# A new order for the opening of a sparse-attention and feed-forward kernel

## The chip, the cores and the metric

The kernel runs on one core of one Trainium2 chip. The metric is the device time of one execution in microseconds (us). A core has five engines that run side by side, each taking its own instructions in order: TensorE (PE, matrix products; loading its weights is shown apart as PEld), VectorE (DVE), ScalarE (ACT), GpSimd (POOL) and SyncE (SP, which here only issues transfers). Transfers are issued from SP's, ACT's and POOL's queues and carried by the same 16 DMA engines. PE writes its products into PSUM, eight banks per partition; everything else lies in SBUF.

## The reference

Eight batches, eight heads, 576 tokens, 64 channels a head. A token attends to those within 32 positions of it; eight global tokens are seen by all and see all. The result, 4608 tokens by 512 channels, goes through a two-layer network.

```python
scores = scale * np.matmul(q, k.transpose(0, 1, 3, 2))
mask = np.abs(pos[:, None] - pos[None, :]) <= window
mask = mask | is_global[:, None] | is_global[None, :]
attn = softmax of scores where mask, else -1e9
x = np.matmul(attn, v), heads side by side   # 4608 x 512
h = x @ w_in                                 # 512 -> 2048
out = (h * np.cos(h)) @ w_out                # 2048 -> 512
```

## The kernel before

**Pairs and units.** The attention is done by pairs of heads, 32 in all; pairs 2s and 2s+1 make half batch s, four pairs a batch. The network is done by tiles of 512 tokens, nine of them. A first-layer unit (`mlp_in`, L754, then `mlp_act`, L765) is four matmuls for 128 of the 2048 inner channels, a cosine on ACT and a product g on DVE; a second-layer unit (`mlp_out`, L790) is four of the sixteen matmuls for 128 tokens. A tile has 16 units of either layer; the fourth of each second-layer group copies its bank out and stores it. That makes 288 units.

**A pair** passes these steps. `k` and `q` (L598, L609): transposes on PE into a bank, and for pairs 0 to 3 small products that pick the global tokens (`pick_globals`, L307), copied out by ACT. `s` (L621 for pairs 0 to 9, L689 for the rest): scores on PE, exponentials on ACT, mask product pm on DVE. `p` (L641, L710): values on PE into pv, of which there is one, then sums, reciprocals and normalised rows xn on DVE. `x` (L670, L734): xn is transposed on PE, DVE copies it into xT, and after a batch's fourth pair POOL writes the eight global columns (L687). `y` (L404): the value rows of the global tokens, from one-hot products, copied by ACT.

**Written order.** The order of all instructions is written out by hand as strings of steps. FRONT covers pairs 0 to 9; MID, FIFTH, SIXTH and ORDER each cover a half batch from number 4 on, issuing the steps of its pairs (letters a, z) and the copies of the next one (c, d); in MID, which stands right behind FRONT, only copies, masks and units. `1` asks for a first-layer unit, `2` for a second-layer unit, `m` and `t` for the two halves of a first-layer unit. A request yields nothing where no unit may run: `one` (L869) needs a ready tile (`ready`: two tiles after FRONT, a third after half batch 5), `two` (L879) needs its inputs and a count below `outs_by`. Other steps: `L` loads a half batch's k and q through POOL, `M` its v through SP, `C` casts v on POOL, `W` loads a quarter of w_in, `O` w_out, `E`, `Y`, `A` gather the global rows, `H` and `g` place them, `f` and `w` are matmuls that only fill time, `n` sums squares on ACT, `Z` builds the steady masks on DVE, `K` casts a half batch from memory to memory, `V` and `U` hold POOL ahead of such a cast until a pair's data is there, `B` (`bring`) transposes k and q and loads v for a half batch through SP.

**Banks.** PSUM banks are taken by tags, each used round by round: s has three, h two, o one, pv two. `k`, `q`, `y` and first-layer units use h; between a `+` and a `-` of the strings every third and fourth first-layer unit uses s. Scores use three of s and the one of o in the opening (`front`), later one of h.

**Half batches 0 to 4** are loaded by POOL with a cast to fp16 (`load_qk`, L275, into three buffers, the third lying in the place of w_out), v as float32 into the two buffers that later hold the products g of tiles 0 and 1. From half batch 5 on everything comes through `K` and `B`. In the loop behind MID, second-layer units are allowed up to 8 (s - 3), and behind the last pair (tail) the remaining units of both layers alternate.

Of the kernel before, what the change touches and what calls it, by code (L numbers as in the profile page):

```python
# [19 lines left out]
P = 128  # L20
NP = H // 2
QB = 56
NB = 11
# [181 lines left out]
def kernel(  # L205
# [31 lines left out]
    nc.sync.dma_start(gidx_all, dview(gi, 0, (0, P), (1, 2 * G)))  # L237
    nc.sync.dma_start(gidx_col, dview(gi, 0, (0, 16), (2, G), (1, 1)))
    nc.sync.dma_start(gidx_row, dview(gi, 0, (2 * G, 1), (1, 2 * G)))
# [67 lines left out]
    def pick_globals(pr, t, src, ones, n, to):  # L307
# [5 lines left out]
        nc.scalar.copy(to, view(t, (0, to.shape[1]), (1, G)))  # L313
# [61 lines left out]

    def next_values(s):

        nc.vector.memset(vn_of(s)[0:64, 0], 0.0)
        load_vn(s)
# [18 lines left out]
    def cast_vn(s):  # L398
        if s > 1:
# [4 lines left out]
    def value_rows(s, part):  # L404

        hs = slice(2 * part, 2 * part + 2)
        rows = ps.tile([P, 512], FP32, tag="h", bufs=2, name="rows")
        for t in range(NK5):
            nc.tensor.matmul(rows[0:G, 0 : 2 * D], one_v[:, t], vn16(s)[:, t, hs, 0:D], start=t == 0, stop=t == NK5 - 1)
        nc.scalar.copy(vn16(s)[0:G, :, hs, 0:D], view(rows[0:G], (0, NK5), (D, 2), (1, D)))  # L410
# [187 lines left out]
    def local_k(pr):  # L598
        to = kw[pr % NK][:, :, G:]
        if pr < 2 * HY:  # L600
            t, g = turned(kn[pr // 2 % NN], pr, KP)
            if pr < PK:
                pick_globals(pr, g, kn[pr // 2 % NN], one_k, KP, k5(pr)[:, :, 0:G])
            nc.scalar.copy(k5(pr)[:, :, G:].rearrange("p n (j r) -> p n j r", r=RW),
                           view(t, (KS // RW, NK5), (1, KS // RW), (QP, RW)))
# [3 lines left out]
    def local_q(pr):  # L609
        to = qb[pr % NK][:, :, G:]  # L610
        if pr < 2 * HY:
            t, g = turned(qn[pr // 2 % NN], pr, QP)
            if pr < PK:
                pick_globals(pr, g, qn[pr // 2 % NN], one_q, QP, q5(pr)[:, 1:, 0:G])
            nc.scalar.copy(qb[pr % NK][:, 0, 0:G], t[:, :, 0])
            nc.scalar.copy(q5(pr)[:, :, G:].rearrange("p n (j r) -> p n j r", r=RW),
                           view(t[:, :, 1:], (KS // RW, NK5), (1, KS // RW), (QP, RW)))
        else:
            nc.vector.tensor_copy(to, view(qT[pr // 2 % 2][:, pr % 2], (QB, NB), (1, QB)))  # L619

    def scores5(pr):  # L621
        kp, qp = k5(pr), qb[pr % NK].rearrange("p j c -> p (j c)")
        pm = pm_of[pr] = work.tile([P, 2 * CN], FP16, tag="pm", name="pm")
        tags = (("s", 3), ("s", 3), ("s", 3), ("o", 1))
# [7 lines left out]
        for h in range(2):  # L632
            e = work.tile([P, 2 * CB], FP16, tag="e", bufs=3)
            nc.scalar.activation(e[:, 0:CA], st[h][:, 0:CA], AF.Exp, scale=scale)  # L634
            nc.vector.tensor_tensor(pm[:, h * CN : h * CN + CA], e[:, 0:CA], mask5[:, 0:CA], ALU.mult)
        e = work.tile([P, 2 * CB], FP16, tag="e", bufs=3)
        for h in range(2):
            nc.scalar.activation(e[:, h * CB : (h + 1) * CB], st[2 + h][:, 0:CB], AF.Exp, scale=scale)  # L638
        nc.vector.tensor_tensor(view(pm[:, CA:], (CN, 2), (1, CB)), view(e, (CB, 2), (1, CB)), view(mask5[:, CA:], (0, 2), (1, CB)), ALU.mult)  # L639
# [49 lines left out]
    def scores(pr):  # L689
# [10 lines left out]
        for h in range(2):  # L700
            e = work.tile([P, 2 * CB], FP16, tag="e", bufs=3)
# [387 lines left out]
```

## Time and profile before

| what | value |
|---|---|
| runs | 353.09, 354.77, 355.42 us; median 354.77 |
| span of the profiled execution, its only time on the page | 353.2 us |
| PE, DVE, ACT, POOL busy | 332.5, 250.1, 245.9, 108.5 us |
| granted PE clock over the span | 0.983 |
| opening, to the end of pair 9's transposes | 58.76 us |
| DMA | 44.58 MB, 126 GB/s on average |

The page gives each engine's busy time; groups of instructions by line, with count, busy time, mean length of one and the idle time ahead of them; who waited for whom; a chain of waits that leads to the last instruction; and a timeline. Stretches of the span can be asked for by themselves. A line of the timeline begins with the start in us and the length, then engine, line of the code, operation, output and input, and in brackets how long the engine stood idle and who released it. Instructions of the same kind that follow on one another are drawn together, with their count.

### The profile page before, as it was taken

To read this page: it belongs to the slowest core of one execution; us is meant where nothing else is said; L and a number is where in the kernel's file an instruction comes from. 1 tells how busy PE (TensorE), PEld (TensorE's weight loads), DVE (VectorE), ACT (ScalarE), POOL (GpSimd) and SP (SyncE) were. 2 spreads that over 40 slices of the span, in tenths; PEclk is the share of its full clock that TensorE was granted. 3 is DMA by queue.
4 is the path that set the end of the run, shared out by engine and by line. 5 is a ranking of instruction groups with operands and counts; after the bars stand their busy time and mean duration, and the time that the engine had idled before them with its cause. 6 is when DMAs were issued, how large, how long until landed. Compare 5 with 4: busy or idle time off the path is not lost.

```text
span 353.2 us, 8389 instructions
## 1 busy us (share of the span) xinstructions
PE 332.5 (94%) x3169; PEld 170.9 (48%) x3169; DVE 250.1 (71%) x611; ACT 245.9 (70%) x423; POOL 108.5 (31%) x221
## 2 busy tenths in 40 slices
PE   7887789999986999999999999999999999999993
PEld 3566675444443444544444545454544444444442
DVE  6565888887586778778787979697878466556410
ACT  8778987884754877777878787777878856644300
POOL 8854847434070507050705071416000100000000
PEclk9898989999999999999999999999999999999998
DMA  5999993999999999999999999999980000100112
GB/s 82 186 149 165 167 192 41 207 164 132 165 147 160 146 199 135 178 118 194 143 187 139 183 139 176 135 161 153 179 93 32 31 32 30 60 32 30 58 63 68
DMA packets 165891, 44.58 MB, mean 126 GB/s; under 512 B 153764, under 2 KB 160996, under 8 KB 165668
## 3 DMA queue, kind: packets, MB, share of 16 engines
q1 hardware_dynamic: 105860, 26.70, 51.2%
q0 software_dynamic: 59984, 17.28, 50.5%
q8 instruction: 27, 0.44, 0.5%
q14 instruction: 20, 0.16, 0.2%
HBM read 44.41 MB, written 19.17 MB: 180 GB/s over the span
## 4 chain that ended last, share of the span: by engine, by line
PE 73%; ACT 8%; DVE 5%; DMA 5%; issue 4%; SPq 3%; POOL 1%; ACTq 0%; POOLq 0%; DVEq 0%
PE po L800 32%; PE ph L762 30%; PE tx L744 2%; DMA kn<-in_k_dram 2%; PE st L699 2%; ACT e L702 2%; PE pv L719 2%; ACT e L634 1%; DMA vw<-vg 1%; ACT e L707 1%; SPq L414 1%; PE po L782 1%; ACT e L638 1%; DVE xn L666 1%; DVE pm L639 1%
## 5 line engine op out<-in xcount | busy, mean ns | idle before, releaser
L762 PE MATMUL ph<-xT,w_in 128*128 128x512 f16 x576 | 140.3, 379 | 1.1 <-DVE g L769 0.3
L768 ACT ACTIVATE cos<-ph,pio 128x512 f16<-128x512 f32 x144 | 97.1, 687 | 62.1 <-PE ph L762 59.9
L800 PE MATMUL po<-w_out,g 128*128 128x512 f16 x560 | 135.4, 379 | 0.0
L769 DVE TENSOR_TENSOR g<-cos,ph 128x512 f16<-128x512 f16 x144 | 95.9, 685 | 42.9 <-ACT cos L768 41.7
L762 PEld LDWEIGHTS <-w_in 128*128 128x128 f16 x576 | 54.2, 97 | 64.6 <-issue 4.6
L800 PEld LDWEIGHTS <-g 128*128 128x128 f16 x560 | 53.7, 98 | 63.6
L703 DVE TENSOR_TENSOR pm<-e,mask 128x512 f16<-128x512 f16 x44 | 18.8, 426 | 19.0 <-ACT e L702 17.7
L702 ACT ACTIVATE e<-st 128x512 f16<-128x512 f32 x44 | 23.9, 594 | 10.0 <-PE st L699 9.8
L980 POOL COPY gate<-xn 1x1 f16<-1x1 f16 x8 | 1.4, 180 | 87.9 <-DVE xn L730 87.9
L752 POOL COPY xT<-xg 128x4 f16 x48 | 15.6, 325 | 32.5 <-DVE xT L747 29.9
L272 POOL DMA_DIRECT2D q<-in_q_dram x11 | 24.0, 2182 | 0.0
L818 ACT ACTIVATE xn<-xn 128x1536 f16<-128x1536 f16 (+1 forms) x16 | 22.5, 1407 | 0.0
L730 DVE TENSOR_TENSOR xn<-pv,r_all 128x768 f16<-128x768 f32 x22 | 21.1, 958 | 1.0
L805 ACT COPY o<-po 128x512 f32<-128x512 f32 x17 | 10.0, 586 | 14.7 <-PE po L800 14.3
L807 DVE COPY o<-po 128x512 f32<-128x512 f32 x18 | 12.4, 690 | 9.0 <-PE po L800 8.5
L272 POOL DMA_DIRECT2D k<-in_k_dram x11 | 18.1, 1645 | 0.9 <-issue 0.9
L768 ACT ACT_TABLE_LOAD x12 | 15.4, 1283 | 0.2
L719 PE MATMUL pv<-vw,pm 128*64 128x65 f16 x484 | 12.7, 197 | 2.7 <-DMA vw<-vg 2.7
L607 DVE COPY kw<-kT 128x1320 f16<-128x1320 f16 x22 | 15.1, 685 | 0.0
L702 ACT ACT_TABLE_LOAD x11 | 14.1, 1283 | 0.2
L699 PEld LDWEIGHTS <-kw 64*128 64x128 f16 x484 | 8.4, 95 | 10.7 <-issue 8.1
L699 PE MATMUL st<-qb,kw 64*128 64x64 f16 x484 | 11.2, 191 | 1.5 <-DVE qb L619 1.1
(185 smaller groups left out, 385.9 us busy)
## 6 DMA issues: line engine op xcount, KB each, us to landing
out_dram<-o SPq DMA_DIRECT2D x35, 256.0 KB
vw<-v SPq DMA_DIRECT2D x32, 165.0 KB
v<-in_v_dram POOLq DMA_DIRECT2D x11, 288.0 KB
k<-in_k_dram POOLq DMA_DIRECT2D x11, 288.0 KB
q<-in_q_dram POOLq DMA_DIRECT2D x11, 288.0 KB
vn<-in_v_dram SPq DMA_DIRECT2D x20, 120.0 KB
w_in<-in_moe_w_in_dram POOLq DMA_DIRECT2D x4, 512.0 KB
w_out<-in_moe_w_out_dram POOLq DMA_DIRECT2D x1, 2048.0 KB
```

Source lines behind the costliest of these rows:

```text
L272: nc.gpsimd.dma_start(dst[s].rearrange("t (h d) -> t h d", h=4), dview(src, base, (D, S), (S * D, 4), (1, D)))
L699: nc.tensor.matmul(st[j // 8 * 2 + h][:, j % 8 * C : j % 8 * C + C], kp[hp, j], qp[hp, j], start=True, stop=True)
L702: nc.scalar.activation(e[:, 0:512], st[h], AF.Exp, scale=scale)
L703: nc.vector.tensor_tensor(view(pm[:, h], (1, 512)), e[:, 0:512], view(mask, (1, 512)), ALU.mult)
L719: nc.tensor.matmul(pv[r0 : r0 + C, j // 6, c0 : c0 + 65], pm[:, h, j], vp[:, j, h], start=True, stop=True)
L730: nc.vector.tensor_tensor(view(xn, (384, 2), (D, 6), (1, D)), view(pv, (512, 2), (65, 6), (1, D)), view(rp, (6, 2), (1, 6), (0, D)), ALU.mult)
L752: nc.gpsimd.tensor_copy(xT[:, :, bass.ds(pool_idx[g] + b * S, 1)], xg[:, :, g : g + 1])
L762: nc.tensor.matmul(ph, w_in16[:, j, f * P : (f + 1) * P], xT[:, j, t * TT : (t + 1) * TT], start=(j == 0), stop=(j == NC - 1))
L768: nc.scalar.activation(cos, ph, AF.Sin, bias=pio2)
L769: nc.vector.tensor_tensor(g, cos, ph, ALU.mult)
L800: nc.tensor.matmul(po, g16[:, f, s * P : (s + 1) * P], w_out16[:, f], start=(f == 0), stop=(f == NF - 1))
L818: nc.scalar.activation(view(xn, (BP * P, 2), (1, n)), view(xn, (BP * P, 2), (1, n)), AF.Square, accum_out=x_sq[:, s : s + 1])
```

## The change

The new opening works in another order and shares its work out differently.

- Half batch 0's k and q come as float32 through SP's and ACT's queues, ahead of the global indices, into `vn32[0]`, and are cast by DVE (k of pairs 0 and 1), ACT (q of pair 0) and POOL (q of pair 1). v of half batches 0 and 1 is loaded at the start; all v loads now share the two places of `vn32[1]`, so each next one follows a cast (`r`).
- FRONT: pairs 0 and 1 are transposed ahead of the first scores; the quarters of w_in (W0 to W3) are issued between pairs 1 and 4, ahead of L3; w_out (`O`) follows pair 5. Sixteen first-layer units (all of tile 0) stand behind pair 5's values, with k, q of pairs 6 and 7 among them; then pairs 6 and 7; then tile 0's sixteen second-layer units, with pairs 8 and 9 among them. Small buffers and the first mask are filled at steps `b`.
- Value rows once per half batch (`value_rows`): one copy of 256 columns by ACT, repeated by POOL. k copies of odd pairs go from ACT to DVE, the eight-column q copy too. The first two mask products of a pair become one.
- MID, FIFTH, SIXTH and ORDER stay; `outs_by` becomes 8 (s - 2), 16 at first.
- In the tail the squares of w_in use places of xn in turn.

```diff
-FRONT = ("M1 s0 E0 C0 E1 L2 k1 q1 w4 s1 y0.0 f4 k2 q2 C1 H0 p0 M2 L3 y0.1 s2 k3 q3 f2 x0 p1 M3 H1 g4 g5 g6 C2 y1.0 s3 g7 L4 I k4 q4 f2 x1 p2 M4 y1.1 s4 "
-         "C3 W0 k5 q5 f2 x2 p3 y2.0 s5 g8 g9 W1 W2 W3 k6 q6 f2 x3 p4 y2.1 s6 C4 Y0 k7 q7 f2 x4 p5 n0 y3.0 s7 k8 q8 f2 x5 p6 y3.1 s8 H2 k9 q9 f2 x6 p7 y4.0 s9 "
-         "x7 p8 y4.1 O m m x8 K5 p9 t t + m m t t x9 -")
+FRONT = ("k1 q1 b0 s0 w4 E0 b2 C0 r2 y0 b3 s1 L2 b4 k2 q2 w2 p0 b1 E1 k3 q3 s2 f2 x0 p1 C1 r3 y1 H0 H1 W0 g4 g5 C2 r4 g6 I "
+         "s3 k4 q4 f2 x1 p2 W1 g7 s4 k5 q5 f2 x2 p3 y2 W2 s5 f2 x3 W3 L3 p4 m m x4 p5 t t 1 1 C3 O g8 g9 1 1 x5 1 1 y3 1 1 1 L4 k6 q6 1 1 k7 q7 1 1 1 F0 s6 s7 "
+         "f2 n0 p6 C4 f2 p7 x6 Y0 H2 x7 2 2 2 2 K5 y4 2 2 k8 q8 2 2 k9 q9 s8 2 2 2 2 s9 p8 2 2 x8 2 2 p9 x9")
...
     def vn_of(s):
-        i = s if s < 4 else 2
-        return view(vn32[i // 2][:, 4 * (i % 2)], (4 * D, NK5), (1, 4 * D))
+        return view(vn32[1][:, 4 * (s % 2)], (4 * D, NK5), (1, 4 * D))
+
+    def load_first(eng, src, pr):
+        to = first_k(pr)[KPAD:KP] if src is k else first_q(pr)
+        eng.dma_start(to, dview(src, 2 * pr * S * D, (RW * D, S // RW), (S * D, 2), (1, RW * D)))
...
-    def value_rows(s, part):
-        hs = slice(2 * part, 2 * part + 2)
+    def value_rows(s):
+        rows, vp = ps.tile([P, 512], FP32, tag="h", bufs=2, name="rows"), vn16(s)
         for t in range(NK5):
+            nc.tensor.matmul(rows[0:G, 0 : 4 * D], one_v[:, t], vp[:, t, :, 0:D], start=t == 0, stop=t == NK5 - 1)
+        nc.scalar.copy(vp[0:G, 0, :, 0:D], view(rows[0:G], (D, 4), (1, D)))
+        nc.gpsimd.tensor_copy(vp[0:G, 1:, :, 0:D], ...)
...
+            copy = nc.vector.tensor_copy if pr % 2 else nc.scalar.copy
...
-        for h in range(2):
-            e = work.tile([P, 2 * CB], FP16, tag="e", bufs=3)
-            nc.scalar.activation(e[:, 0:CA], st[h][:, 0:CA], AF.Exp, scale=scale)
-            nc.vector.tensor_tensor(pm[:, h * CN : h * CN + CA], e[:, 0:CA], mask5[:, 0:CA], ALU.mult)
+        for i, (c, n) in enumerate(((0, CA), (CA, CB))):
+            e = work.tile([P, 2 * CA], FP16, tag="e", bufs=3)
+            for h in range(2):
+                nc.scalar.activation(e[:, h * n : (h + 1) * n], st[2 * i + h][:, 0:n], AF.Exp, scale=scale)
+            nc.vector.tensor_tensor(view(pm[:, c:], (CN, 2), (1, n)), view(e, (n, 2), (1, n)), view(mask5[:, c:], (0, 2), (1, n)), ALU.mult)
...
+        for t in ((k, nc.sync), (q, nc.scalar)):
+            load_first(t[1], t[0], 0)
+        nc.sync.dma_start(gidx_all, dview(gi, 0, (0, P), (1, 2 * G)))
+        nc.sync.dma_start(gidx_col, dview(gi, 0, (0, 16), (2, G), (1, 1)))
+        load_first(nc.scalar, q, 1)
+        load_first(nc.sync, k, 1)
...
+        cast_first(nc.vector.tensor_copy, k, 0)
+        cast_first(nc.scalar.copy, q, 0)
+        cast_first(nc.gpsimd.tensor_copy, q, 1)
         build_band()
+        cast_first(nc.vector.tensor_copy, k, 1)
+        build_ones()
         index_rows(1)
...
-            outs_by[0] = 8 * (s - 3)
+            outs_by[0] = 8 * (s - 2)
```

More of the change, by code (lines that the diff above doesn't have):

```diff
@@ L402, in cast_vn @@
         nc.gpsimd.tensor_copy(new[:, :, :, 0:D], old)
-    def value_rows(s, part):
-        hs = slice(2 * part, 2 * part + 2)
-        rows = ps.tile([P, 512], FP32, tag="h", bufs=2, name="rows")
+    def value_rows(s):
+        rows, vp = ps.tile([P, 512], FP32, tag="h", bufs=2, name="rows"), vn16(s)
         for t in range(NK5):
-            nc.tensor.matmul(rows[0:G, 0 : 2 * D], one_v[:, t], vn16(s)[:, t, hs, 0:D], start=t == 0, stop=t == NK5 - 1)
-        nc.scalar.copy(vn16(s)[0:G, :, hs, 0:D], view(rows[0:G], (0, NK5), (D, 2), (1, D)))
+            nc.tensor.matmul(rows[0:G, 0 : 4 * D], one_v[:, t], vp[:, t, :, 0:D], start=t == 0, stop=t == NK5 - 1)
+        nc.scalar.copy(vp[0:G, 0, :, 0:D], view(rows[0:G], (D, 4), (1, D)))
+        first = vp[0:G, 0, :, 0:D]
+        nc.gpsimd.tensor_copy(vp[0:G, 1:, :, 0:D], bass.AP(first.tensor, first.offset, [first.ap[0], [0, NK5 - 1], *first.ap[1:]]))
     def load_vg(pr):
@@ L700, in scores @@
         for h in range(2):
-            e = work.tile([P, 2 * CB], FP16, tag="e", bufs=3)
+            e = work.tile([P, 2 * CA], FP16, tag="e", bufs=3)
             nc.scalar.activation(e[:, 0:512], st[h], AF.Exp, scale=scale)
             nc.vector.tensor_tensor(view(pm[:, h], (1, 512)), e[:, 0:512], view(mask, (1, 512)), ALU.mult)
-        e = work.tile([P, 2 * CB], FP16, tag="e", bufs=3)
+        e = work.tile([P, 2 * CA], FP16, tag="e", bufs=3)
         n = (NB - 8) * C
@@ L824, in weight_squares @@
         if j == 0:
[L825 to L826 removed]
+            w_sq[c] = view(work.tile([P, 2, BP, P], FP16, tag="xn", bufs=4, name="wsq"), (512, 3), (1, 512))
+        at = w_sq[c][:, (0, 1, 2, 1)[j]]
+        nc.scalar.activation(at, w_in16[:, j, c * 512 : (c + 1) * 512], AF.Square)
         if j:
[L828 removed]
+            nc.vector.tensor_tensor(w_sq[c][:, 0], w_sq[c][:, 0], at, ALU.add)
     def weight_norms(c):
@@ L885, in two @@
                 mlp_out(*outs_q.pop(0))
-    outs_by = [0]
+    outs_by = [16]
     ready = [0, 0]
```

106 lines of the change are left out of this document (57 added, 49 removed).

## The prediction

> **What bounds the kernel now.** First the head of the page: TensorE (PE) is busy for 94% of the span. Then busy time by stage, cut where a pair's scores begin, and where the opening ends (58.76, the end of pair 9's transposes in the chain of waits).
>
> ```profile
> span 353.2 us, 8389 instructions
> PE 332.5 (94%) x3169; PEld 170.9 (48%) x3169; DVE 250.1 (71%) x611; ACT 245.9 (70%) x423; POOL 108.5 (31%) x221
> 58.48 0.28 PE tx L678 x5
> 0.00:58.76 58.76, 49.17 (x910) 34.32 (x911) 41.58 (x153) 48.94 (x104) 38.26 (x79) 0.91 0.90 142
> 58.76:88.66 29.90, 29.58 (x137) 13.11 (x136) 25.57 (x59) 21.31 (x33) 14.68 (x19) 1.00 1.34 161
> 88.66:102.18 13.52, 12.01 (x141) 6.17 (x141) 9.62 (x24) 8.90 (x15) 4.40 (x7) 1.00 1.41 161
> 102.18:122.62 20.44, 17.64 (x167) 8.75 (x168) 14.10 (x32) 13.85 (x27) 8.05 (x20) 1.00 1.50 151
> 139.76:156.91 17.15, 17.09 (x165) 8.38 (x164) 13.97 (x32) 13.07 (x21) 6.49 (x16) 1.00 1.56 149
> 294.83 1.03 PE L762 MATMUL ph<-xT,w_in 128*128 128x512 f16 x4
> 296.56 1.03 PE L762 MATMUL ph<-xT,w_in 128*128 128x512 f16 x4
> ```
>
> The columns of a stage are its length, then busy PE, PEld, DVE, ACT, POOL, then the granted clock, the DMA share and GB/s. From 58.76 on PE is nearly full: in the steady stage 17.09 of 17.15 us. Only the opening has room: 9.6 us of idle PE in 58.76, with ACT busy 48.9. One second-layer unit lies between the last two rows, so a unit of four matmuls costs (296.56 - 294.83)/2 = 0.865 us. All 288 units are needed in either order, so **the time changes only by the idle PE**, and a moved unit pays only where PE would have stood still.
>
> **The yardstick.** The old opening holds 4 first-layer units, the new one 16 and 16 second-layer units, 28 more. It breaks even if its last transposes (x9, time T) end at 58.76 + 28 x 0.865 = 83.0, if nothing is lost behind it.
>
> **Up to the first unit.**
>
> ```profile
> L634 ACT ACTIVATE e<-st 128x488 f16<-128x488 f32 x20 | 10.3, 561 | 2.8 <-PE t L319 1.6 <-PE st L631 1.1
> L638 ACT ACTIVATE e<-st 128x384 f16<-128x384 f32 x20 | 8.6, 481 | 0.2 <-PE st L631 0.2
> L410 ACT CAST vw<-rows 8x640 f16<-8x640 f32 x10 | 6.9, 687 | 3.3 <-PE rows L409 3.3
> L604 ACT COPY kw<-bank 128x600 f16<-128x600 f16 x10 | 6.6, 655 | 0.3 <-PE tx L678 0.3
> L615 ACT COPY qb<-bank 128x8 f16<-128x8 f16 x10 | 1.8, 179 | 0.0
> 3.83 0.18 DVE L475 CAST df<-d_i 128x192 f32<-128x192 int32 x1
> 5.53 0.09 DVE L484 MEMSET band<- 8x32 uint32 x1
> 7.59 1.04 ACT L917 ACTIVATE vn<-vn 8x1024 uint32<-8x1024 uint32 x1
> 10.85 1.04 ACT L634 ACTIVATE e<-st 128x488 f16<-128x488 f32 x2 [0.46 <-PE t L319]
> 13.08 1.29 POOL L402 CAST vw<-vn 128x1280 f16<-128x1280 f32 x1 [0.67 <-DMA vn<-in_v_dram]
> 34.01 1.01 ACT L634 ACTIVATE e<-st 128x488 f16<-128x488 f32 x2
> 42.52 2.44 POOL L687 COPY xT<-xg 128x4 f16 x8
> ```
>
> A pair's exponentials start every (34.01 - 10.85)/5 = 4.63 us, set by ACT. Per pair the change takes off ACT half a k copy (0.33; the odd ones go to DVE), the small q copy (0.18), and most of the value rows: 0.69 becomes one copy of 256 columns for two pairs, between 0.18 and 0.69, taken as 0.35, so 0.5 less a pair. That is 1.0: the interval is 3.6 if all of it is felt, 4.6 if none. The start does not gain. Half batch 0 now comes as float32 from SP's and ACT's queues and is cast by three engines. No row shows such a cast on DVE; the nearest, POOL's of 1280 columns, takes 1.29, and I take 0.5 to 1.1. DVE's order is k0's cast, the band (3.83 to 5.62, 1.8 us), k1's cast, then the one-hot rows for which PE's picks of pair 0 wait, about 9.3; with q0, k1 and q1 behind them in PE's queue, the first scores come near 12 and the exponentials at 12.7 instead of 10.85. The second pair's scores stand behind y0, hence behind b2 (1.04 on ACT) and C0 (1.29 on POOL). So I take 3.8: pair 5's exponentials at 12.7 + 5 x 3.8 = 31.7 (30.7 to 35.8), ended at 33.8. On DVE pair 5's mask product and then x3's copies come next (1.3), then POOL's eight copies for the global tokens (2.0 to 2.4): the first unit, which reads them, starts at **37** (35 to 41).
>
> **Sixteen units in a row.** They take their banks from tag h, which has two; s banks are only used while the plus mark holds, which is not in the new opening.
>
> ```profile
> 109.01 1.90 PE L762 MATMUL ph<-xT,w_in 128*128 128x512 f16 x8
> 110.08 0.69 ACT L768 ACTIVATE cos<-ph,pio 128x512 f16<-128x512 f32 x1 [0.46 <-PE ph L762]
> 110.80 0.69 DVE L769 TENSOR_TENSOR g<-cos,ph 128x512 f16<-128x512 f16 x1
> ```
>
> A bank is held from 109.01 to 111.49, 2.5 us, so two banks give a unit every 1.27 us and not every 0.865. No row has three such units running: 0.865 is one bound, 1.27 the other, and I take 1.27, the row's own. k6, q6, k7, q7 and y3 use the same two banks, about 1.3 us each. 21 uses: (16 x 2.53 + 5 x 1.3)/2 = 23.5, and 2.5 at the head, where the products of the first two units stand on DVE behind pair 5's normalisation. **26 us** (24 to 28; 16 by the other bound) to pair 6's scores at 63.
>
> Then one pair of chains stands alone: the last cosine 0.9, an ACT table load 1.28, pair 6's exponentials 2.0, pair 7's scores and exponentials 2.4, its mask 0.7, p6 and p7 on one pv with 1.3 of normalisation behind each, x7: **11 us** (9 to 12) with 4 of PE work. At 74 the second layer begins. Sixteen units (13.8) with pairs 8 and 9 and y4 (6.1 of PE) cover each other, 1.6 more for x9's wait: **21.5**. T = 37 + 26 + 11 + 21.5 = **95.5**, 12.5 past break-even.
>
> The queues don't set this.
>
> ```profile
> 54.00:56.00 2.00, 1.81 (x21) 1.00 0.00 1
> 57.06 1.21 POOL L897 DMA_DIRECT2D w_out<-in_moe_w_out_dram  x1
> 72.59 0.95 POOL L335 DMA_INDIRECT vg<-in_v_dram,gidx_rows  x1 [5.29 <-DMA w_out<-in_moe_w_out_dram]
> ```
>
> Before, all half batches and w_in had landed by 54 (1 GB/s after it). In the new order L3, behind W0 to W3 in POOL's queue, is wanted at 54 and L4 after 77; w_out takes at most 15.5, is issued near 40 and wanted at 74. W3 and L3 are both issued behind x3's eight copies. Cost 0; if that cover is gone, up to 5.
>
> **Behind the opening.** MID keeps its list, but only tile 1's 16 first-layer units are left for it (26 and 8 before).
>
> ```profile
> L769 DVE TENSOR_TENSOR g<-cos,ph 128x512 f16<-128x512 f16 x29 | 18.7, 681 | 3.8 <-ACT cos L768 3.7
> 83.39 0.18 POOL L389 COPY gate<-qb 1x1 f16<-1x1 f16 x1 [7.61 <-DVE qb L619]
> 93.24 1.33 SPq L284 DMA_TRANSPOSE kT<-k  x1
> 96.36 1.29 SPq L285 DMA_TRANSPOSE qT<-q  x1
> 102.18 0.67 PE L699 MATMUL st<-qb,kw 64*128 64x64 f16 x22 [1.12 <-DVE qb L619]
> 122.62 0.49 PE L699 MATMUL st<-qb,kw 64*128 64x64 f16 x22
> 123.43 1.28 ACT L702 ACT_TABLE_LOAD   x1
> 124.72 1.09 ACT L702 ACTIVATE e<-st 128x512 f16<-128x512 f32 x2
> ```
>
> (1) PE ends MID's units at T + 13.8. DVE has 16 products (10.9), the steady masks (about 3 of the second stage's 25.57) and pair 10's copies (1.0), and starts 1.8 late: pair 10's scores at T + 17.5. **Lost 4** (3 to 5). (2) The gate of half batch 6 waits for pair 10's copy, also at T + 17.3. From that gate to pair 12's scores it took 102.18 - 83.39 = 18.8 before, with PE waiting 1.12 at the end. Queued behind the gate on POOL are the casts, behind them SP's transposes. With half batch 5's loads out of the way I take 14.5, T + 31.8. Between x9 and these scores lay 44 units before and lie 24 now; 20 units less would put them 102.18 - 58.76 - 20 x 0.865 = 26.1 behind T, and with (1) 30.1. **Lost 2** (0 to 6). (3) Stage 7 has tile 2's first 8 units only, so one second-layer unit and not four stands between two pairs' scores; the second needs banks that the first pair's exponentials free 3.2 us on (124.72 + 1.09 - 122.62), 1.3 of it covered. **Lost 2.5** (1.5 to 4). Stage 6's own waits I leave as they are. In all 8.5.
>
> **Sum.** 353.2 + 12.5 + 8.5 = 374.2 for the span, the only time that the profile gives of its execution. The runs' median, 354.77, is 1.6 above it: **376 us**.
>
> **Rivals.** *PE's pace in the row of units*: were a unit 0.865 there, the block would take 16, so 366. Against it: two banks. 0.18. *It wins*: the units fill all 9.6 us of idle PE in the opening, and stages 5 to 7 don't starve: 345. It decides at T: below 83 - 8.5 = 74.5 the time falls, above it rises. The relief of ACT speaks for it; two banks and the lone pairs 6 and 7 against. 0.05, and 0.05 for a T near 75, within 1%. *The clock*:
>
> ```profile
> 7.87 1.04 PE L319 MATMUL t<-ones 128*128 128x512 f16 x4
> 13.35 1.81 PE L319 MATMUL t<-ones 128*128 128x512 f16 x4
> 24.00:26.00 2.00, 0.77 (x26) 1.00 1.03 161
> 28.00:30.00 2.00, 1.99 (x30) 0.50 1.28 212
> ```
>
> Half clock follows stretches in which PE was half idle, and makes four matmuls 1.81 instead of 1.04. Were the row of units caught in it, a unit would take 0.43 longer, 16 of them 7 us: 383. PE is busy for two thirds of that block, which speaks against it. 0.12. The Trainium skill (TensorE: Matmul & The Clock Gate, A second HAM failure mode: psum-queue depth-cycling) tells of just this: cycling through PSUM banks leaves small gaps that drop the clock again and again. The halves here agree with it; whether gaps of 0.8 us do it no row here shows. *Half batch 6 as slow as before* (18.8, and its value loads late again): 4 more, 380. 0.1. *The change does not do what it says* about w_in: W3 and L3 wait for the same copies, so that order alone is worth nothing; it is part of the forecast. The forecast itself: 0.5.
>
> **Range and chances.** The bounds of the forecast's terms give T from 35 + 24 + 9 + 21 = 89 to 41 + 28 + 12 + 21.5 = 102.5, and 4.5 to 15 lost behind it: 365 to 389. The first rival's middle, 366, lies in it, and its lower half reaches down to 362. 362 to 389 leaves out about 0.2, the winning case among it. A measurement of this kernel tells 1% from no change: faster 0.05, same 0.05, slower 0.90.
>
> **What would show it.** Right: x3's global copies end at 35 to 41 and release the first unit; PE waits for DVE's g within the row of units, at 1.27 a unit; pair 6's scores near 63; x9 ends near 95; PE idle 3 to 5 us ahead of pair 10's scores, waiting for DVE; a gap between pairs 14 and 15. Wrong: units at 0.865 in a row, x9 before 80, or PE full from pair 5 on.

## The result, and the profile after

The changed kernel took **438.25 us** (437.2 to 439.89), the kernel before 354.28 beside it: a ratio of 1.236, interval [1.231, 1.241]. The forecast was 376, at most 389. The direction was right; of the 84 us lost only a quarter was foreseen.

The head of the changed kernel's page, with two of its groups of instructions; behind the last bar stands the idle time ahead of a group, and what ended most of it:

```profile
span 436.3 us, 8250 instructions
PE 358.5 (82%) x3132; PEld 179.7 (41%) x3132; DVE 254.9 (58%) x614; ACT 223.4 (51%) x400; POOL 118.2 (27%) x225
L806 PE MATMUL po<-w_out,g 128*128 128x512 f16 x560 | 150.1, 406 | 24.4 <-DVE o L813 23.3
L768 PE MATMUL ph<-xT,w_in 128*128 128x512 f16 x576 | 144.3, 386 | 7.9 <-DVE g L775 4.0
```

PE is busy for 82% of the span and not 94. Of the 83.1 us that the span grew by, 57.1 are idle PE (77.8 against 20.7) and 26.0 are PE busy for longer (358.5 against 332.5) with 37 matmuls fewer: its granted clock over the span is 0.904 and not 0.983. The largest single idle time stands ahead of *second-layer* matmuls: 23.3 us of waiting for DVE's copy `o`, which the prediction does not mention. Busy time by stage (columns as in the prediction), cut at the first unit, pair 6's scores, the second layer's first unit, the end of x9 (T), pair 12's scores, and from there at a half batch's first scores:

```profile
0.00:53.67 53.67, 35.44 (x544) 25.07 (x545) 29.63 (x105) 24.58 (x51) 33.34 (x56) 0.67 0.71 131
53.67:83.00 29.33, 23.23 (x163) 10.87 (x164) 13.55 (x28) 11.19 (x19) 7.67 (x12) 0.86 0.85 133
83.00:94.33 11.33, 6.46 (x76) 5.00 (x76) 6.19 (x16) 6.63 (x12) 3.49 (x4) 0.63 0.03 7
94.33:124.14 29.81, 24.74 (x206) 11.61 (x205) 8.73 (x23) 8.22 (x15) 13.52 (x23) 0.85 0.51 73
124.14:160.37 36.23, 26.35 (x197) 12.17 (x195) 25.10 (x66) 19.17 (x34) 9.02 (x12) 0.91 1.05 99
...
179.78:195.81 16.03, 13.16 (x146) 6.61 (x146) 13.11 (x30) 11.76 (x20) 4.87 (x9) 1.00 1.50 163
195.81:216.15 20.34, 17.32 (x165) 8.29 (x165) 14.06 (x33) 12.24 (x21) 6.61 (x16) 1.00 1.35 135
```

By the prediction's own yardstick (0.865 us a unit moved):

| stretch | before, corrected for units | after | lost | foreseen |
|---|---|---|---|---|
| start to T | 83.0 | 124.14 | 41.1 | 12.5 |
| T to pair 12's scores | 43.42 - 20 units = 26.1 | 36.23 | 10.1 | 6 |
| pair 12's to pair 16's scores | 37.58 - 5 units = 33.3 | 35.44 | 2.2 | 2.5 |
| pair 16's scores to the end | 213.44 - 3 units = 210.8 | 240.49 | 29.7 | 0 |

The four losses make 83.1, the difference of the spans. Two lines are far off: the opening and the steady stages. The last row of the fence shows a steady stage: 20.34 us with 17.32 of PE in it, where the kernel before took 17.15 with 17.09.

What happens in a steady stage. PE's timeline of the kernel before, from a half batch's first scores:

```profile
156.91 0.49 PE L699 MATMUL st<-qb,kw 64*128 64x64 f16 x22
157.34 3.63 PE L800 MATMUL po<-w_out,g 128*128 128x512 f16 x16
160.90 0.49 PE L699 MATMUL st<-qb,kw 64*128 64x64 f16 x22
```

The same place in the changed kernel:

```profile
216.15 0.49 PE L705 MATMUL st<-qb,kw 64*128 64x64 f16 x22
216.58 1.04 PE L806 MATMUL po<-w_out,g 128*128 128x512 f16 x4
220.74 2.75 PE L806 MATMUL po<-w_out,g 128*128 128x512 f16 x12 [3.13 <-DVE o L813]
223.43 0.49 PE L705 MATMUL st<-qb,kw 64*128 64x64 f16 x22
```

And DVE in that stretch of the changed kernel:

```profile
218.80 0.91 DVE L709 TENSOR_TENSOR pm<-e,mask 128x512 f16<-128x512 f16 x2 [1.22 <-ACT e L708]
219.73 0.36 DVE L714 TENSOR_TENSOR pm<-e,mask 128x384 f16<-128x384 f16 x1
220.00 0.68 DVE L813 COPY o<-po 128x512 f32<-128x512 f32 x1
```

Four second-layer units stand between two pairs' scores. Before, they were the four of one group (sixteen matmuls in a row), and the group's copy came when DVE had time. Now the first of them *ends* a group and the next three begin another. There is one bank with tag o, so these three need it copied out; the copy is issued behind the first pair's mask products, and they wait for exponentials. The wait takes 2.6 to 3.1 us, once in each of eight stages, 23.3 in all, and six of the stages take 20.3 to 20.4 us. In the other two half clock follows the wait, and they take 22.98 and 21.82 (granted clock 0.85 and 0.92). The cause is a count: stage 7 has three second-layer units to give and not eight, so every later half batch begins five units away from a group's edge.

The opening, by PE's timeline of the changed kernel:

```profile
12.83 0.59 PE L309 MATMUL bank<-one_k,kn 75*64 75x8 f16 x16 [5.25 <-DVE one_k L302]
18.18 0.91 PE L640 MATMUL st<-qb,kw 64*128 64x136 f16 x10
...
24.36 0.91 PE L640 MATMUL st<-qb,kw 64*128 64x136 f16 x10
...
31.47 0.91 PE L640 MATMUL st<-qb,kw 64*128 64x136 f16 x10
...
39.01 1.02 PE L640 MATMUL st<-qb,kw 64*128 64x136 f16 x10
...
48.10 0.55 PE L640 MATMUL st<-qb,kw 64*128 64x136 f16 x10
...
53.67 0.59 PE L768 MATMUL ph<-xT,w_in 128*128 128x512 f16 x1 [2.98 <-POOL xT L693]
...
142.12 0.77 PE L705 MATMUL st<-qb,kw 64*128 64x64 f16 x22 [4.16 <-DVE qb L628]
...
160.37 0.72 PE L705 MATMUL st<-qb,kw 64*128 64x64 f16 x22 [3.81 <-issue]
```

The first scores come at 18.2, the next three at intervals of 6 to 7.5, pair 5's at 48.1, and the first unit at 53.7 instead of 37. What PE waits for at 12.83 stands in DVE's timeline of the changed kernel:

```profile
6.29 0.62 DVE L944 CAST kn<-vn 75x1024 f16<-75x1024 f32 x1
...
11.35 1.17 DVE L944 CAST kn<-vn 75x1024 f16<-75x1024 f32 x1 [2.77 <-DMA vn<-in_k_dram]
12.44 0.20 DVE L301 TENSOR_TENSOR one_q<-tok_i,gidx_all 128x64 f16<-128x64 int32 x1
12.57 0.21 DVE L302 SCALAR_TENSOR_TENSOR one_k<-tok_i,gidx_all 128x64 f16<-128x64 int32 x1
```

DVE stands idle for 2.8 us until k of pair 1 has landed, with the one-hot rows that pair 0 needs behind that cast. In the row of units the wait is the one foreseen (for `g`), and so is the one ahead of pair 10's scores (4.16, for `qb`).

### The profile page after: what moved, and what is told of

Read it like the earlier page. It is cut to its first block, busy times and chain, and to the rows that moved or that the text cites. A ratio compares the mean times of both kernels' runs of the same rounds, so it can differ in the third digit from the quotient of the medians.

```text
span 436.3 us, 8250 instructions
## 1 busy us (share of the span) xinstructions
PE 358.5 (82%) x3132; PEld 179.7 (41%) x3132; DVE 254.9 (58%) x614; ACT 223.4 (51%) x400; POOL 118.2 (27%) x225
## 4 chain that ended last, share of the span: by engine, by line
PE 63%; ACT 13%; DVE 9%; issue 7%; POOL 4%; DMA 2%; another core or an unknown queue 1%; POOLq 0%; SPq 0%; ACTq 0%; DVEq 0%
PE po L806 29%; PE ph L768 26%; ACT e L708 4%; ACT L708 3%; ACT cos L774 3%; DVE g L775 2%; PE tx L750 2%; DMA vn<-in_k_dram 2%; ACT e L644 1%; DVE o L813 1%; PE pv L725 1%; PE st L705 1%; DVE pm L709 1%; ACT e L713 1%; POOL vw L405 1%
## 5 line engine op out<-in xcount | busy, mean ns | idle before, releaser
L806 PE MATMUL po<-w_out,g 128*128 128x512 f16 x560 | 150.1, 406 | 24.4 <-DVE o L813 23.3
L768 PE MATMUL ph<-xT,w_in 128*128 128x512 f16 x576 | 144.3, 386 | 7.9 <-DVE g L775 4.0
L774 ACT ACTIVATE cos<-ph 128x512 f16<-128x512 f32 x144 | 84.7, 597 | 84.1 <-PE ph L768 78.3
L806 PEld LDWEIGHTS <-g 128*128 128x128 f16 x560 | 55.8, 103 | 98.8 <-issue 41.7
L709 DVE TENSOR_TENSOR pm<-e,mask 128x512 f16<-128x512 f16 x44 | 18.7, 426 | 48.1 <-ACT e L708 46.8
L645 DVE TENSOR_TENSOR pm<-e,qT 128x976 f16<-128x976 f16 (+1 forms) x20 | 14.5, 737 | 11.7 <-ACT e L644 11.1
L644 ACT ACTIVATE e<-st 128x488 f16<-128x488 f32 (+1 forms) x40 | 18.1, 550 | 4.9 <-PE st L640 4.7
L705 PE MATMUL st<-qb,kw 64*128 64x64 f16 x484 | 11.6, 194 | 9.5 <-DVE qb L628 4.2
L811 ACT COPY o<-po 128x512 f32<-128x512 f32 x17 | 10.0, 589 | 16.4 <-PE po L806 16.3
L269 POOL DMA_DIRECT2D k<-in_k_dram x11 | 18.2, 1651 | 0.2 <-issue 0.2
```

What stands on the lines that cost most here:

```text
L269: nc.gpsimd.dma_start(dst[s].rearrange("t (h d) -> t h d", h=4), dview(src, base, (D, S), (S * D, 4), (1, D)))
L644: nc.scalar.activation(e[:, h * n : (h + 1) * n], st[2 * i + h][:, 0:n], AF.Exp, scale=scale)
L705: nc.tensor.matmul(st[j // 8 * 2 + h][:, j % 8 * C : j % 8 * C + C], kp[hp, j], qp[hp, j], start=True, stop=True)
L709: nc.vector.tensor_tensor(view(pm[:, h], (1, 512)), e[:, 0:512], view(mask, (1, 512)), ALU.mult)
L768: nc.tensor.matmul(ph, w_in16[:, j, f * P : (f + 1) * P], xT[:, j, t * TT : (t + 1) * TT], start=(j == 0), stop=(j == NC - 1))
L774: nc.scalar.activation(cos, ph, AF.Sin, bias=pi / 2.0)
```

## The experiments

The kernel before ran beside every one of them (354.3 to 355.3). The unaltered changed kernel, run again beside a part of them, took 431.6, so the altered ones are set against that.

> The changed kernel unaltered, on this chip, so that the other runs beside it have their own yardstick. Expected 428 to 440 us: the two altered kernels whose openings are word for word its own ended them at 118 us, where its profile ended at 124.

No edit. It took **431.56** (431.01 to 432.1): first unit 51.97, T 117.53, the same waits. The 6.7 us between its two measurements lie mostly in the stretch with pairs 8 and 9, to which I come back at the end. Two measurements of one kernel can lie as far apart as this, so a smaller difference between the times of two runs counts below only where the stages of their traces show it.

**1. The groups of the second layer.** Shifted in the kernel before, aligned in the changed one:

```diff
 # kernel before
-            outs_by[0] = 8 * (s - 3)
+            outs_by[0] = 8 * (s - 3) - (5 if s > 6 else 0)
 # changed kernel
-            outs_by[0] = 8 * (s - 2)
+            outs_by[0] = 8 * (s - 2 - (s > 6))
```

> The kernel before, with one number changed: from half batch 7 on five second-layer units fewer are allowed, so that stage 7 gives three and every later stage begins with the last unit of a group instead of the first. Theory (a group's bank is copied out by DVE behind the mask products, and tag o has one bank, so PE waits in the middle of the four units between two pairs' scores): stages 8 to 15 grow from 17.15 to about 20.3 us, 8 x 3.2 = 25, and stage 7 loses 3; about 382 us. Rival (the longer stages of the changed kernel are left over from its opening: clock, late loads of half batch 6): stages 8 to 15 stay at 17.15, 355 to 358 us.

> The changed kernel, with no second-layer unit in stage 7 (three before), so that every later stage begins with the first unit of a group again. Theory of the shifted groups: stages 8 to 15 fall from 20.3 back to 17.2 us, 8 x 3.2 = 25 less, and stage 7, which has only eight units, gains nothing; about 412 us. Rival (left over from the opening): 435 to 440 us.

Measured: **388.33** (ratio 1.095) and **403.8** (1.137), where 382 and 412 were expected. This one line makes the old kernel 33 us slower and the new one 28 us faster, with the opening as it was in each. The waits of PE, in the kernel before with shifted groups (columns: in total, times, longest):

```profile
PE po L800 <- DVE o L807: 25.3, 8, 3.2
```

and PE's timeline of the changed kernel with aligned groups, where sixteen matmuls run through again:

```profile
224.05 0.49 PE L705 MATMUL st<-qb,kw 64*128 64x64 f16 x22
224.48 3.63 PE L806 MATMUL po<-w_out,g 128*128 128x512 f16 x16
228.04 0.49 PE L705 MATMUL st<-qb,kw 64*128 64x64 f16 x22
```

The period of its steady stages is 17.1 us. That the shift costs this, and not the new opening as such, is shown from both sides.

**2. Banks in the row of units.**

```diff
-... f2 x3 W3 L3 p4 m m x4 p5 t t 1 1 C3 ... k7 q7 1 1 1 F0 s6 s7
+... f2 x3 W3 L3 p4 + m m x4 p5 t t 1 1 C3 ... k7 q7 1 1 1 - F0 s6 s7
```

> The changed kernel, with the plus and minus marks around its row of sixteen units, so that every third and fourth unit takes a bank of tag s. Theory (two banks set the pace): the row from the first unit (53.7) to pair 6's scores (83.0) shrinks from 29.3 to about 21 us, about 430 us. Rival (ACT and DVE or the clock set the pace): no change of the row, 438 us.

Measured: **426.36** (1.201). From the first unit (51.64) to pair 6's scores (73.3) it takes 21.7 us and not 29: the two banks were the bound, as the prediction has it. Part of PE's timeline of this run, then of the changed kernel:

```profile
62.86 2.76 PE L768 MATMUL ph<-xT,w_in 128*128 128x512 f16 x12
```

```profile
70.26 1.89 PE L768 MATMUL ph<-xT,w_in 128*128 128x512 f16 x8 [0.26 <-DVE g L775]
```

Three units run through without a gap; with two banks a wait for `g` stands ahead of every second one.

The same for the second layer, whose odd groups take an s bank when the minus mark is moved behind x9:

```diff
-... k7 q7 1 1 1 - F0 s6 s7 ... p9 x9")
+... k7 q7 1 1 1 F0 s6 s7 ... p9 x9 -")
```

> The changed kernel with s banks in the row of first-layer units (426.4 us) and now also for every other group of tile 0's second layer. Theory: that stretch is set by the chains of pairs 8 and 9 and by the half clock, not by the one output bank: 425 to 428 us, the stretch from the first second-layer unit to the last transposes still 25 us. Rival: the output bank holds PE there too: 3 us less in that stretch, 423 us.

Measured: **426.47** (1.201), with 25 us for that stretch as before. The output bank is not its bound.

**3. Half batch 6.** Its cast was put ahead of pair 10's copies, without its hold.

```diff
-... 1 2 2 g10 g11 kc qc V10 K6 2 2 ...
+... 1 2 2 K6 g10 g11 kc qc 2 2 ...
```

> The changed kernel, with the cast of half batch 6 issued ahead of pair 10's copies and not held back by them. Theory (the chain gate, cast, transposes, copies makes pair 12's scores late, 36.2 us behind the opening's end where its work takes 30): these scores come 4 to 5 us earlier, about 433 us. Rival (they wait for the masks and copies on DVE): no earlier, 438 us.

Measured: **428.77** (1.208); pair 12's scores at T + 33.6, with the hold T + 33.8 (run with aligned groups) and T + 33.6 (again). The cast was issued some 27 us earlier and nothing came of it. So the gate, on which I had hung term (2), does not set this stretch. What PE shows there in this run is sixteen second-layer matmuls at 1.6 us a unit instead of 0.87, and waits for `xn` between two pairs that have few units to cover them:

```profile
136.88 6.24 PE L806 MATMUL po<-w_out,g 128*128 128x512 f16 x16
...
146.93 0.51 PE L750 MATMUL tx<-ident,xn 128*128 128x128 f16 x6 [1.91 <-DVE xn L736]
```

**4. Why the first unit is late.** Six theories were tried, one after the other. POOL first: value rows copied by ACT to all places again, the clears of three buffers (two of them POOL's) put on ACT at the start.

```diff
-        nc.scalar.copy(vp[0:G, 0, :, 0:D], view(rows[0:G], (D, 4), (1, D)))
-        first = vp[0:G, 0, :, 0:D]
-        nc.gpsimd.tensor_copy(vp[0:G, 1:, :, 0:D], ...)
+        nc.scalar.copy(vp[0:G, :, :, 0:D], view(rows[0:G], (0, NK5), (D, 4), (1, D)))
...
+        for t in (qn[2][64:QP], kn[2][0:KPAD]):
+            nc.scalar.memzero(flat(t))
```

> The changed kernel, with POOL's queue relieved in the opening: the value rows are copied to all five places by ACT as before (POOL's repeating copies of 1.03 us, which wait for ACT, are gone), the two buffers of half batch 2 are cleared by ACT at the start (1.8 us each on POOL), and the clearing that half batch 0's cast waits for stands on ACT ahead of the first scores. Theory (POOL's in-order queue sets the opening: gathers, casts and loads stand behind waits of others): the first unit starts 6 to 9 us earlier than 52 to 54, and the total falls by as much. Rival (PE at half clock sets it): the first unit moves by less than 2 us.

Measured: **430.9** (1.214); first unit 48.7 instead of 52.0, T 2.3 earlier. POOL's queue explains 3.3 us of the 15 by which the first unit is late (52.0, forecast 37). The whole time moved by 0.7, too little to tell.

Then the clock, by matmuls that compute nothing:

```diff
+        warm(30)
         local_k(0)
+        warm(14)
         local_q(0)
-FRONT = ("k1 q1 b0 s0 w4 E0 ... k2 q2 w2 p0 b1 E1 k3 q3 s2 f2 x0 p1 C1 r3 y1 H0 ...
+FRONT = ("k1 q1 b0 s0 w14 E0 ... k2 q2 w10 p0 b1 E1 k3 q3 s2 f9 x0 p1 C1 r3 y1 w10 H0 ...
```

> The changed kernel, with 77 more matmuls that compute nothing where PE stands idle before the first unit. Theory of the half clock (0.50 from 12 to 44 us stretches PE's work there): granted clock near 1.00 up to the first unit, which starts 4 to 6 us earlier. Rival (POOL's queue sets the opening): clock up, first unit within 2 us of the unaltered kernel's.

Measured: **435.71** (1.228). Busy time of this run, up to pair 0 and from there to the first unit:

```profile
0.00:18.00 18.00, 16.34 (x155) 7.75 (x156) 6.90 (x25) 5.61 (x9) 12.14 (x20) 1.00 0.78 160
18.00:53.00 35.00, 26.48 (x472) 18.74 (x472) 23.90 (x81) 18.82 (x42) 21.04 (x37) 0.95 0.68 118
```

The clock was granted in full or nearly so, against 0.72 and 0.64 there in the changed kernel, and the first unit stayed at 52.7. That does not clear the half clock, for the added matmuls stand in PE's own queue: pair 0's scores came at 18.6 instead of 16.4. From pair 1's scores to pair 2's, in the changed kernel run again and then in this run:

```profile
22.58:29.70 7.12, 7.12 (x161) 5.96 (x161) 3.04 (x13) 3.57 (x9) 6.26 (x6) 0.50 0.67 113
24.27:30.19 5.92, 5.92 (x169) 4.38 (x169) 2.28 (x7) 3.46 (x9) 5.23 (x5) 1.00 0.56 108
```

PE is busy without a gap in both. Without the matmuls that only fill time (1.03 and 2.33 us of these stretches) the same work takes 6.1 us at half clock and 3.6 at full, an estimate from these rows. So here PE at half clock is the bound, at a price of some 2.5 us, and the added matmuls used up most of what the clock gave. Ahead of pair 3's scores PE waits 1.85 us for POOL in the unaltered kernel, so it is open how much sooner the first unit would come at full clock without them; that was not tried.

Then the start. On top of POOL's relief, the one-hot rows ahead of k1's cast, and pair 0's scores ahead of pair 1's transposes:

```diff
-FRONT = ("k1 q1 b0 s0 w4 ...
+FRONT = ("b0 s0 k1 q1 w4 ...
-        cast_first(nc.vector.tensor_copy, k, 1)
         build_ones()
+        cast_first(nc.vector.tensor_copy, k, 1)
```

> The changed kernel with POOL relieved as in the run before (430.9 us, first unit at 48.7), and now also with pair 0's scores ahead of pair 1's transposes and the one-hot rows ahead of k1's cast. Theory: the 5 us that PE stands waiting for the one-hot rows, and pair 1's transposes, run through to the first unit: pair 0's scores near 12.5 instead of 16.5, the first unit near 44.5, about 427 us. Rival: pairs 1 to 3 wait for POOL's and DVE's own queues, so only pair 0 is earlier, and the first unit stays at 48 to 49, about 431 us.

Measured: **428.31** (1.207). Pair 0's scores come at 13.7 instead of 16.5, the first unit at 48.0 instead of 48.7: nearer to the rival. Of the 2.7 us gained at pair 0, 1.2 are left at pair 1 and 0.7 at the first unit.

Then the copies that the change moves from ACT to DVE. Alone, in the kernel before:

```diff
-            nc.scalar.copy(k5(pr)[:, :, G:].rearrange("p n (j r) -> p n j r", r=RW),
+            copy = nc.vector.tensor_copy if pr % 2 else nc.scalar.copy
+            copy(k5(pr)[:, :, G:].rearrange("p n (j r) -> p n j r", r=RW),
...
-            nc.scalar.copy(qb[pr % NK][:, 0, 0:G], t[:, :, 0])
+            nc.vector.tensor_copy(qb[pr % NK][:, 0, 0:G], t[:, :, 0])
```

> The kernel before, with one part of the change alone: the k copies of odd pairs and the small q copies go from ACT to DVE. Theory (ACT sets the pace of its opening, 4.63 us a pair; 0.5 us a pair less on it): opening 3 to 5 us shorter, 350 to 352 us. Rival (DVE, or the order of copies between two engines, takes the place): 354 to 357 us.

Measured: **359.21** (1.012, interval [1.003, 1.020]), so slower by 1.2% where I had expected faster; its opening ends at 63.05 instead of 58.76. ACT's waits in that opening point to the reason, and the kernel before has no such line:

```profile
ACT qb L617 <- DVE qb L616: 7.3, 9, 1.6
```

ACT's large q copy stands behind the small one of the same bank, which now stands in DVE's queue behind mask products. Nor had ACT been full in the old opening. Busy time of the kernel before from pair 0's scores to pair 6's (ACT is the fourth figure behind the length):

```profile
10.44:37.82 27.38, 22.45 (x517) 17.31 (x516) 16.86 (x58) 21.66 (x53) 15.84 (x28) 0.88 1.03 164
```

Undone in the changed kernel, on the base of the run before:

```diff
-            copy = nc.vector.tensor_copy if pr % 2 else nc.scalar.copy
+            copy = nc.scalar.copy
-            nc.vector.tensor_copy(qb[pr % NK][:, 0, 0:G], t[:, :, 0])
+            nc.scalar.copy(qb[pr % NK][:, 0, 0:G], t[:, :, 0])
```

> The changed kernel with POOL relieved and pair 0's scores first (428.3 us, first unit at 48.0), now with all k copies and the small q copies on ACT again. Theory: the small q copy stands behind mask products on DVE, and ACT's large q copy, the next transposes and scores wait for it; without that the first unit comes 3 to 4 us earlier, near 44.5, and the whole near 425. Rival: ACT, given 0.5 us more a pair, becomes the bound, and the first unit is no earlier, 48 to 50, 428 to 430 us.

Measured: **425.0** (1.199), the first unit at 45.4, T at 110.1 (114.0). Scores of pairs 4 and 5 in this run:

```profile
35.58 0.55 PE L638 MATMUL st<-qb,kw 64*128 64x136 f16 x10 [0.95 <-POOL d_i L966]
...
39.05 0.55 PE L638 MATMUL st<-qb,kw 64*128 64x136 f16 x10
```

3.5 us apart, and 4.6 in the base. So between these two pairs the part that I had booked as a gain of 0.5 us is a loss of about 1. The first unit comes 2.6 us earlier in all, of which 2.0 are there at pair 0 already. From pair 1's scores to pair 2's this run again takes 7.12 us, all of them busy PE at a granted clock of 0.50.

The joined mask products, apart again on the same base:

```diff
-        for i, (c, n) in enumerate(((0, CA), (CA, CB))):
...
+        for h in range(2):
+            e = work.tile([P, 2 * CA], FP16, tag="e", bufs=3)
+            nc.scalar.activation(e[:, 0:CA], st[h][:, 0:CA], AF.Exp, scale=scale)
+            nc.vector.tensor_tensor(pm[:, h * CN : h * CN + CA], e[:, 0:CA], mask5[:, 0:CA], ALU.mult)
...
```

> The same base (428.3 us, first unit at 48.0), now with the first two mask products of a pair apart again, each behind its own exponential. Theory: the joined product starts one exponential (0.45 to 0.56 us) later, on a chain of six pairs: the first unit 1 to 3 us earlier, 45 to 47. Rival: the mask is not on the chain: no change, 48.

Measured: **429.27** (1.210), first unit 47.2, of which 0.3 were there at pair 0 already: no difference that can be told.

Last, pair 1's scores ahead of the value rows, on the base with copies on ACT:

```diff
-FRONT = ("b0 s0 k1 q1 w4 E0 b2 C0 r2 y0 b3 s1 L2 ...
+FRONT = ("b0 s0 k1 q1 w4 s1 E0 b2 C0 r2 y0 b3 L2 ...
```

> The run with copies on ACT (425.0 us, pair 1's scores at 19.65, first unit at 45.4), now with pair 1's scores written ahead of the gathers, the value cast and the value rows. Theory: pair 1's wait for the values is passed on to all later pairs: its scores near 15.5, the first unit 3 to 4 us earlier, near 42, 421 to 422 us. Rival: pair 0's values product needs the value rows all the same, and the later pairs stand behind it: the first unit within 1 us of 45.4, 424 to 425 us.

Measured: **433.82** (1.225). Pair 1 is 1.7 earlier, but pair 2 at 27.5 (26.8) and the first unit at 46.2 (45.4): the rival's line. Pair 0's value product waits for the value rows all the same. 5.6 of the 8.8 us that the whole lost lie between pair 6's scores and T (41.9 instead of 36.3), a stretch which this edit does not touch.

**5. The second layer in the opening.** Left to the loop behind it, with aligned groups:

```diff
-         "f2 n0 p6 C4 f2 p7 x6 Y0 H2 x7 2 2 2 2 K5 y4 2 2 k8 q8 2 2 k9 q9 s8 2 2 2 2 s9 p8 2 2 x8 2 2 p9 x9")
+         "f2 n0 p6 C4 f2 p7 x6 Y0 H2 x7 K5 y4 k8 q8 k9 q9 s8 s9 p8 x8 p9 x9")
-    outs_by = [16]
+    outs_by = [0]
-            outs_by[0] = 8 * (s - 2)
+            outs_by[0] = 8 * (s - 3)
```

> The changed kernel without the sixteen second-layer units in the opening; they come in the loop behind it, allowed up to 8 (s - 3) as in the kernel before, so the groups are aligned (to be set beside the aligned run, 403.8 us). Theory: the stretch with pairs 8 and 9 takes 25 us for 13.8 us of units; bare, the two pairs take 12 to 14, so the opening ends 11 to 13 us earlier, 13.8 of units come back behind it, and 8 of them cover MID's waits: 398 to 404 us. Rival: the units fill time that the pairs need anyway: the opening ends only 4 us earlier, and 410 us or more.

Measured: **395.53** (1.115), against 403.8 with aligned groups and the second layer where the change puts it. The opening ends 10 us earlier, and the sixteen units do not cost as much behind it. That part of the change costs 8.3 us.

**6. Together.** First the first three remedies with aligned groups, then also copies on ACT and the second layer out, then also pair 1's scores moved. The edits are those shown above.

> All four edits together: aligned groups in the second layer, s banks in the row of units, POOL relieved, pair 0's scores first. Theory: the costs found lie in different places and add up: 431.6 less 27.8 (aligned), 5 to 7.6 (banks), 0.7 and 4, so 392 to 394 us, with the end of the opening near 102. That would be 16 to 18 above my forecast of 376, to be looked for in the opening. Rival: what the opening gains is given back behind it, where half batch 6 comes no sooner: 398 to 404 us.

> All that was found together: s banks in the row of units, POOL relieved, pair 0's scores first, copies on ACT, and tile 0's second layer behind the opening with aligned groups. Theory: the costs add: 390.9 (all mended), less 8.3 for the second layer (403.8 to 395.5), less 3 for the copies: 378 to 381 us, the opening's end near 92. What then stays above the kernel before, some 25 us, is the order itself. Rival: with the end of the opening early enough half batch 6 and MID's products become the next bound: 385 us or more.

> The run with all that was found together (383.1 us), now with the same move of pair 1's scores. Theory: what the opening gains is kept: 379 to 380 us. Rival: no gain, 382 to 384 us. Either way over 20 us above the kernel before would stay with the order itself.

Measured: **390.85** (1.102), **383.06** (1.082) and **385.79** (1.086); pair 1's move gains nothing here either. Taken from the single runs, 431.6 - 27.8 (groups) - 5.2 (banks) - 0.7 (POOL) - 2.6 (first scores) = 395.3 for the first, and 390.9 was measured; less 3.3 (copies) and 8.3 (second layer) it makes 383.7 for the second, and 383.1 was measured. So the costs add up to within some 4 us. That the second sum fits to 0.6 is partly luck: from the first run to the second it has 11.6, and 7.8 was measured. Busy time of the second of these runs up to the first unit, the row of units, and pairs 6 to 9:

```profile
0.00:45.36 45.36, 31.61 (x545) 22.16 (x545) 27.37 (x96) 30.59 (x62) 27.33 (x51) 0.77 0.86 157
45.36:66.83 21.47, 19.88 (x163) 9.39 (x164) 11.74 (x25) 12.53 (x22) 6.60 (x11) 0.93 1.10 176
66.83:93.46 26.63, 16.64 (x215) 12.06 (x215) 12.97 (x35) 15.12 (x28) 15.80 (x24) 0.60 0.60 64
```

Its opening holds 12 units more than the old one, so it would break even at 58.76 + 12 x 0.865 = 69.1 and ends at 93.5. These 24.4 us are nearly all of the 26.1 by which its span (379.3) exceeds 353.2. PE stands idle for 25.3 us in it (9.6 before), 13.8 of them ahead of the first unit and 10.0 among pairs 6 to 9. These two stretches run at a granted clock of 0.77 and 0.60, and PE is busy for 68.1 us in the whole opening, where the old one's 49.2 and 12 units would make 59.6. So 15.7 us of the loss are idle PE and some 8.6, by this estimate, the lower clock. That it is the order itself is an argument and was not tried: the old opening runs ten pairs without a break, a pair every 4.5 us (scores of pair 0 at 10.4, of pair 9 at 50.6); the new one breaks off after six for a row of units, and the last four then take 26.6 us by themselves. No version here came nearer to the kernel before than this 383.1.

## Why the prediction was right or wrong

The sum was 374.2 for the span. Its terms against the trace, T 28.6 too low (95.5 to 124.14), T to pair 12's scores 4.1, the two stages behind it 0.3 too high, and the steady stages 29.7, make 436.3.

- **The step that failed most: "In all 8.5", which prices everything from pair 16's scores on at nothing, and the yardstick behind it, that a unit costs 0.865 wherever it stands and that "the time changes only by the idle PE".** I counted stage 7's units (one second-layer unit between two scores) and priced the gap there, 2.5, which the trace bears out: 2.2 for the two stages. I did not carry the count on to the stages behind it. The rows to see it by lay in the kernel before: sixteen second-layer matmuls in one row of the timeline, tag o with one bank, a group of four. The price is 29.7 in the trace, 28 and 33 in the two runs. Nor is it only idle PE: over the whole span 26.0 of the 83.1 us are PE busy for longer with nearly the same matmuls at a lower clock, for which the sum has no term.
- **Up to the first unit: 37 (35 to 41), measured 53.7, and 52.0 when run again.** The mechanism at its end was right (x3's copies on POOL, 2.04, release it). Wrong were the start, scores at 18.2 and not near 12, because k1's load lands near 11.3 and the one-hot rows stand behind its cast; and the interval, 6.0 and not 3.8. The old interval was put down to ACT, but from pair 0's scores to pair 6's ACT was busy for 21.7 of 27.4 us. The relief of ACT was booked by what ACT no longer does; what the moved copy waits for on DVE, and who waits for it, was not asked. That one was a gain turned into a loss (3.3 us of the whole, 2.6 of the first unit; 4 in the kernel before). POOL's extra clears and copies, for which the sum has no term, took another 3.3 of the first unit, and the late start 0.7. The other 8 us are the slower first three pairs. Neither the joined masks nor the place of pair 1's scores is their cause; PE at half clock is the bound from pair 1's scores to pair 2's, some 2.5 us; for the rest no cause was shown.
- **Sixteen units in a row: 26, measured 29.3.** Right in kind, as the run with s banks shows; the head was mis-sized (7.45 us from the first unit to the third, 5.0 in the sum), in part because the first two units ran at half clock (3.57 for 1.90).
- **Pairs 6 and 7: 11, measured 11.3. Right.**
- **Second layer with pairs 8 and 9: 21.5, measured 29.8, and 25.3 when run again.** Mis-sized: I took the units at the full clock, and behind the lone pairs (clock 0.63) the first four ran at half of it (6.27 us for 3.5). x9's wait, 1.6, came as 1.46.
- **Pair 10's scores at T + 17.5: measured T + 18.0, with the wait for DVE's `qb`. Right**, 4.16 for "lost 4".
- **Pair 12's scores at T + 31.8: measured T + 36.2**, and T + 33.6 when run again. The gate is not the cause.
- **The rivals.** PE's pace in the row of units needs more banks; with them 21.7 us, not 16. "It wins" had 74.5 as its point, and T was 124. The clock was named for the wrong place: the row of units kept 0.86, the opening ahead of it had 0.67, and there PE at half clock was the bound for at least one pair. The Trainium skill (TensorE: Matmul & The Clock Gate, A second HAM failure mode: psum-queue depth-cycling) has the clock swing where matmul groups cycle through PSUM banks with small gaps; the trace does not agree here. Four stretches of 4 us of the row of units:

```profile
54.00:58.00 4.00, 4.00 (x20) 2.02 (x19) 0.18 (x1) 1.19 (x2) 4.00 (x5) 0.50 0.74 115
62.00:66.00 4.00, 4.00 (x12) 1.46 (x11) 1.38 (x2) 1.72 (x3) 0.00 (x0) 0.57 1.23 198
66.00:70.00 4.00, 3.42 (x20) 1.51 (x19) 3.09 (x7) 1.87 (x4) 0.00 (x0) 1.00 1.24 208
70.00:74.00 4.00, 3.20 (x29) 1.45 (x29) 1.58 (x3) 1.81 (x4) 2.43 (x3) 1.00 0.82 111
```

Half clock followed the waits of 2.98 and 2.05 us ahead of the first and the third unit. From 66 on every second unit waits, and these gaps of 0.3 to 0.6 us left the clock at 1.00.

The range was too narrow because it was put together from the bounds of the terms that I had; the largest loss was in none of them.

**What stays open.** The stretch from pair 6's scores to T took 41.1 in the first run of the changed kernel, 36.6 when run again, and 41.9 in the run with pair 1's scores moved. In the first of these PE and DVE stood still together ahead of the last of pair 8's scores, and the trace names no engine for it; in the third PE stood still there for shorter times (0.96, 0.47 and 0.51 us without a releaser, and 1.09 for ACT's `qb`). PE's timeline of the first run of the changed kernel, then DVE's:

```profile
109.47 0.32 PE L640 MATMUL st<-qb,kw 64*128 64x192 f16 x3 [2.62 <-issue]
```

```profile
108.63 0.78 DVE L609 COPY kw<-bank 128x600 f16<-128x600 f16 x1 [4.30 <-remote]
```

Half batch 5's cast and six gathers run just then. They do so in the second run of the same kernel too (1.62 MB within 16 us in either), where PE waits 0.21 us at this place, so they alone do not make the wait. The cause is open.

## What to carry to other kernels

When a change moves work out of a loop, follow the count to the end of the loop: a group that shares one bank is cheap only while its edge falls where the bank's reader has time, and a shift of one unit costs in every round. Before booking a copy moved to another engine as a gain, ask what stands ahead of it in the new queue and which later instruction of the old engine waits for it. An engine that waits may also come back slower: look at its busy time as well as its idle time. Whether units strewn among the chains of this opening would do better than sixteen in a row was not tried.

## What the runs showed of the hardware that was not expected

- Filling PE's idle time with 79 idle matmuls kept the granted clock at 1.00 and 0.95 up to the first unit, against 0.72 and 0.64, and the first unit came no earlier (52.7, 52.0): the added matmuls took the time themselves.
- The same float32 cast of 75 x 1024 on DVE took 0.62 us at 6.3 and 1.17 at 11.35; with a constant as bias, the cosine took 597 ns, and 687 with a tile. The first I have no cause for; the second came with the change and was not tried by itself.
